# A fused attention-and-MLP kernel: block 1's half of the seven-product groups, one group quarter in SBUF, and a new instruction sequence

## The chip, the cores and the metric

The kernel runs on one core of a Trainium2 chip. TensorE (PE) multiplies into PSUM, which has eight banks of 128 x 512 fp32; VectorE (DVE) and ScalarE (ACT) read and write PSUM and SBUF, GpSimd (POOL) works on SBUF alone; SyncE (SP), ACT and POOL issue DMAs. The metric is the device time in microseconds (us), the median of three executions.

## The reference

Linear attention with random features, then a two-layer MLP with a hard-swish between its layers. With 8 batches, 8 heads, 576 tokens, head size 64, 128 features, hidden size 512 and inner size 2048 it computes, cut to what matters:

```
phi(x) = exp(x' @ omega.T - |x'|^2/2 - max) / sqrt(m)      # x' = x * 64**-0.25
kv, z  = sum over tokens of phi(k) v,  sum of phi(k)
x      = (phi(q) kv) / (phi(q) z + 1e-6)                   # then heads side by side: 4608 x 512
h      = x @ w_in                                          # 4608 x 2048
g      = h * clip(h + 3, 0, 6) / 6
out    = g @ w_out                                         # 4608 x 512
```

## The kernel before

**Tiling.** One batch's first 512 tokens make a block: block b is batch b for b = 0 to 7. The 64 tokens left over of each batch are woven together into block 8. For each block the MLP has a first product, h = x @ w_in, whose activation goes to the tile `gT`, and a second product, g @ w_out. The attention of batch b+1 is interleaved with the MLP of block b, so that PE has work from both.

**Plain first product.** `mm1` (L1083) makes one row of 128 inner units for 512 tokens: four matmuls 128 x 512 into one PSUM bank. ACT then computes relu(h/6 + 0.5) into `tsb` (L1089), and DVE makes min(tsb, 1) * h into `gT` (L1091). Block 0 goes by half blocks (`mm1_half`, L1302).

**First product by seven products.** `mm1_quad` (L1248) makes a group of four such rows, two neighbouring ones in each half of w_in, by seven products of quarter matrices (Strassen's scheme in Winograd's form) in place of eight. A group takes seven times four matmuls 128 x 256, called qa, qw, qb, qy, qz, qc and qd, into four banks X, Y, Z and W. It needs three copies of a bank (q1, q2, q3; ACT or DVE, L543 and L544), two additions on DVE (q4, L1273; q5, L1276), then four times ACT's relu (qr0 to qr3, L1284) and four times DVE's last step (qg0 to qg3, L1286). q3 copies bank W into an SBUF tile `p7`, of which there are two in turn; q5 adds Z and `p7` back into bank W, and qr2 and qg2 read the third quarter there. The scheme also needs sums of w_in, made once per half of the groups (`input_sums`: W3, W2, W4 and W1, the last of which overwrites a quarter of w_in), and four sums of x in each block (`x_sums`: X1 to X4). All such sums are SBUF additions in `combine` (L1343), on DVE or POOL.

`FIRST7 = (7, 2)` and `QUAD = (7, 2)` say from which block on the two halves of the groups (inner units f with f // 4 = 0 and 1) go by seven products: the first half from block 7, the second from block 2. Block 1 is all plain.

**Second product.** From block 1 on it goes by seven products as well (`products`, L1415, 128 x 256), with sums S1 to S4 of `gT` (`token_sums`, `last_sum`; again `combine`, L1343), and with additions on DVE at L1431.

**Attention.** Loads are DMAs: k and q for batches 1 and up are cast on the way by POOL's DMA queue (L643), v comes by SP's. From batch 2 on k and q are transposed by SP's DMA queue (L777), and the attention's output x too (`xT`, L1059, and `xS`). `K`, `Q` and, from batch 3 on, the burst `R` (four row tiles, L796 and L799) project on omega; ACT takes exp (L815, L824; L847, L864 in the early batches), DVE the maxima (L820, L851). `vc` (L970 on POOL, L972 on ACT) scales v, `vcl` (L886 POOL, L889 ACT) v's left over tokens, and `kv` and `num` (L986, L1014) do the sums. DVE divides (L1030).

**What sets the order.** The program builds a list of operations with the data that they read and write. `ORDER` gives, for every engine, the sequence of its operations by their place in that list, so it also says which of several allowed engines does one. `schedule` walks these lists with a table of durations and landing times; what that walk decides is which PSUM bank an operation gets, where idle PE matmuls on the tile `fill` (L597) go in the first microseconds, and in which order waits are recorded. It can't change the sequence of an engine. Each engine then runs its list in order and stands still when the next operation has to wait.

Of the kernel before, what the change touches and what calls it, by code (L numbers as in the profile page):

```python
# [16 lines left out]
EV0 = (("ACT","DVE"), ("ACT","DVE"), ("POOL", "ACT"), {"k": ("POOL", "ACT", "DVE"), "q": ("POOL", "ACT","DVE")})  # L17
# [4 lines left out]
        14, 121, 115, 117, 131, 138, 159, 147, 119, 141, 150, 144, 156, 135, 127, 153, 123, 125, 176, 129, 133, 174,  # L22
        166, 170, 172, 168, 188, 190, 203, 162, 178, 205, 164, 218, 193, 180, 220, 233, 208, 195, 235, 210, 407, 248,
        395, 223, 401, 198, 396, 238, 402, 397, 240, 408, 403, 398, 245, 225, 409, 404, 410, 213, 413, 416, 243, 228,
        271, 419, 291, 251, 422, 425, 428, 431, 275, 281, 434, 277, 437, 279, 318, 440, 443, 273, 309, 446, 315, 306,
        289, 285, 449, 312, 287, 297, 300, 586, 596, 303, 326, 320, 597, 336, 576, 294, 587, 330, 577, 588, 328, 283,
        578, 598, 332, 324, 589, 322, 599, 357, 579, 566, 359, 567, 362, 344, 580, 590, 568, 346, 334, 383, 569, 570,
        571, 349, 370, 385, 591, 365, 572, 581, 375, 372, 388, 600, 601, 592, 582, 583, 352, 391, 593, 573, 378, 602,
        603, 617, 505, 620, 614, 623, 466, 469, 475, 478, 635, 490, 472, 629, 632, 487, 481, 647, 484, 659, 644, 507,
        501, 653, 638, 497, 493, 668, 503, 499, 665, 662, 495, 650, 779, 511, 509, 531, 519, 780, 521, 536, 533, 524,  # L30
        789, 555, 782, 783, 560, 557, 790, 543, 712, 545, 548, 792, 793, 692, 795, 798, 799, 705, 796, 816, 810, 813,
        719, 819, 825, 828, 840, 831, 834, 845, 842, 844, 802, 863, 847, 803, 868, 849, 851, 865, 744, 870, 867, 732,
        987, 874, 737, 997, 734, 988, 872, 768, 756, 746, 1003, 749, 761, 990, 758, 998, 773, 770, 991, 1000, 1001, 900,
        1004, 1006, 1007, 913, 1018, 1024, 1021, 920, 1010, 1027, 1033, 927, 1039, 1050, 1048, 1036, 1011, 1042, 1053,
        1071, 1052, 1073, 1055, 1076, 1057, 1075, 952, 1059, 1078, 1080, 1195, 940, 976, 1082, 942, 957, 1196, 945, 954,
        1205, 964, 1198, 969, 966, 1199, 1206, 978, 981, 1121, 1208, 1209, 1108, 1214, 1215, 1128, 1229, 1232, 1226,
        1241, 1135, 1235, 1244, 1256, 1247, 1250, 1261, 1258, 1260, 1211, 1263, 1279, 1212, 1265, 1284, 1267, 1283,
        1281, 1218, 1286, 1403, 1404, 1290, 1148, 1160, 1219, 1150, 1165, 1288, 1184, 1162, 1153, 1406, 1413, 1414,
        1329, 1189, 1407, 1186, 1172, 1416, 1174, 1177, 1336, 1417, 1419, 1420, 1316, 1422, 1423, 1440, 1437, 1434,
        1452, 1464, 1449, 1443, 1466, 1468, 1469, 1458, 1455, 1471, 1426, 1473, 1427, 1343, 1475, 1487, 1356, 1611,  # L40
        1491, 1492, 1358, 1380, 1489, 1361, 1494, 1382, 1368, 1612, 1370, 1498, 1496, 1373, 1614, 1392, 1621, 1615,
        1622, 1537, 1394, 1397, 1385, 1624, 1625, 1544, 1627, 1628, 1551, 1630, 1634, 1631, 1524, 1635, 1642, 1645,
        1672, 1648, 1651, 1657, 1660, 1677, 1674, 1676, 1663, 1564, 1576, 1679, 1566, 1578, 1569, 1666, 1681, 1695,
        1581, 1683, 1588, 1699, 1600, 1590, 1697, 1593, 1700, 1722, 1702, 1602, 1723, 1605, 1704, 1706, 1753, 1732,
        1725, 1776, 1726, 1733, 1757, 1758, 1755, 1781, 1735, 1760, 1736, 1762, 1764, 1778, 1780, 1783, 1741, 1799,
        1742, 1787, 1785, 1738, 1804, 1801, 1824, 1803, 1806, 1822, 1739, 1808, 1810, 1826, 1827, 1745, 1876, 1829,
        1746, 1831, 1833, 1878, 1845, 1881, 1880, 1901, 1846, 1883, 1899, 1885, 1848, 1904, 1903, 1849, 1887, 1924,
        1906, 1922, 1908, 1855, 1927, 1926, 1856, 1910, 1929, 1945, 1858, 1931, 1949, 1933, 1950, 1859, 1861, 1947,
        1862, 1952, 1864, 1978, 1865, 1956, 1968, 1969, 1868, 1869, 1954, 1979, 1984, 1971, 1981, 1982, 1985, 1972,
        1988, 1989, 1997, 2003, 2000,  # L50
    ],
    "SP": [
        0, 18, 22, 33, 20, 23, 26, 25, 24, 27, 28, 32, 29, 30, 31, 262, 260, 261, 465, 464, 462, 463, 461, 459, 460,
        393, 585, 688, 575, 689, 685, 691, 690, 605, 595, 539, 527, 563, 551, 564, 686, 687, 801, 805, 896, 897, 893,
        898, 899, 740, 752, 764, 776, 894, 895, 1105, 777, 1013, 1106, 1104, 1107, 1009, 948, 960, 972, 984, 1103, 1102,
        1101, 1309, 1312, 1217, 1313, 985, 1314, 1315, 1221, 1311, 1168, 1156, 1192, 1180, 1310, 1520, 1429, 1193, 1523,
        1522, 1521, 1425, 1518, 1364, 1400, 1388, 1376, 1401, 1517, 1519, 1572, 1633, 1584, 1637, 1596, 1608, 1609,
        1744, 1748, 1867, 1871, 1992, 1993, 2005,
    ],
    "ACT": [  # L60
        21, 19, 118, 139, 132, 148, 142, 160, 145, 136, 151, 128, 124, 154, 184, 167, 157, 134, 187, 202, 169, 175, 173,
        171, 163, 179, 232, 219, 177, 165, 234, 181, 209, 411, 405, 399, 417, 244, 420, 292, 426, 414, 429, 423, 276,
        435, 278, 432, 319, 438, 444, 310, 441, 447, 307, 316, 286, 313, 301, 450, 304, 321, 298, 327, 295, 337, 329,
        356, 331, 333, 343, 323, 358, 381, 345, 325, 382, 368, 335, 371, 353, 618, 594, 621, 584, 506, 615, 604, 476,
        470, 624, 473, 479, 636, 467, 633, 488, 648, 630, 491, 485, 645, 530, 508, 660, 502, 482, 654, 639, 504, 669,
        666, 500, 498, 494, 496, 651, 512, 663, 520, 554, 781, 541, 510, 542, 784, 544, 713, 717, 715, 718, 699, 704,
        701, 698, 695, 693, 697, 703, 708, 706, 817, 711, 811, 710, 814, 720, 722, 724, 725, 820, 829, 826, 743, 841,
        832, 835, 843, 852, 727, 864, 728, 869, 854, 856, 866, 745, 858, 875, 767, 733, 755, 754, 881, 879, 989, 769,
        757, 877, 992, 906, 907, 903, 912, 901, 905, 909, 911, 914, 918, 916, 919, 1025, 1019, 1022, 925, 926, 923,
        1028, 921, 1034, 930, 932, 939, 928, 1040, 1051, 933, 1049, 1037, 1043, 1054, 1072, 1060, 1074, 1077, 1062,  # L70
        1064, 1083, 1066, 1085, 941, 977, 1089, 963, 1087, 1197, 965, 1200, 1126, 1124, 1127, 1122, 1120, 1117, 1115,
        1119, 1114, 1111, 1109, 1131, 1113, 1230, 1134, 1233, 1133, 1129, 1227, 1242, 1138, 1141, 1136, 1236, 1245,
        1257, 1248, 1159, 1140, 1251, 1262, 1259, 1280, 1268, 1270, 1272, 1274, 1285, 1291, 1282, 1295, 1297, 1149,
        1161, 1183, 1170, 1293, 986, 1171, 1185, 1334, 1330, 1335, 1332, 1408, 1337, 1339, 1341, 1342, 1325, 1317, 1323,
        1319, 1327, 1441, 1321, 1322, 1328, 778, 1435, 1438, 1465, 1453, 1450, 1444, 1467, 1476, 1470, 1459, 1355, 1456,
        1480, 1478, 1346, 1344, 1482, 1348, 1357, 1349, 1499, 1493, 1381, 1490, 1369, 1503, 1613, 1505, 1501, 1393,
        1616, 1543, 1538, 1542, 1540, 1194, 1545, 1549, 1547, 1550, 1557, 1554, 1556, 1552, 1527, 1525, 1531, 1529,
        1535, 1533, 1643, 1530, 1673, 1646, 1536, 1649, 1652, 1658, 1661, 1678, 1675, 1563, 1684, 1664, 1565, 1577,
        1599, 1686, 1696, 1667, 1589, 1690, 1601, 1707, 1698, 1701, 1688, 1724, 1711, 1713, 1709, 1754, 1727, 1777,
        1765, 1756, 1610, 1782, 1769, 1767, 1771, 1779, 1792, 1788, 1790, 1794, 1805, 1802, 1811, 1823, 1815, 1813,  # L80
        1825, 1828, 1817, 1834, 1840, 1836, 1838, 1879, 1882, 1888, 1847, 1902, 1890, 1892, 1911, 1905, 1894, 1925,
        1850, 1923, 1913, 1915, 1928, 1917, 1934, 1946, 1938, 1940, 1951, 1936, 1957, 1948, 1961, 1963, 1959, 1970,
        1991, 1996, 1995, 1994, 1999, 2002,
    ],
    "DVE": [
# [75 lines left out]
class Prog:  # L161
# [47 lines left out]
    def schedule(self):  # L209
# [83 lines left out]
        while any(lists.values()):  # L293
# [33 lines left out]
            else:  # L327
                free[e] = st + occ
                o.end = free[e]
                if e in o.port:  # L330
                    shared[0] = o.end - (0.07 if e == "POOL" else 0.0)
# [89 lines left out]
def _emit(nc, es, q, k, v, omega, w_in, w_out, out):  # L421
# [112 lines left out]
    def dvet(n):  # L534
        return 0.07 + n / 960.0
# [420 lines left out]
    def pair(b, m, t):  # L956
# [11 lines left out]
        def e_vc(E):  # L968
            if E is not nc.scalar:
                return E.tensor_tensor(vcm[:, :, 0:D], v32[:, m, :, :], cbc, ALU.mult)  # L970
# [641 lines left out]
```

## Time and profile before

| what | value |
|---|---|
| median of 3 runs | 302.28 us (301.57 to 302.39) |
| the profiled execution | 302.46 us, span 300.6 us |
| PE busy | 292.2 us, 97% |
| PE weight loads busy | 222.1 us, 74% |
| DVE busy | 271.4 us, 90% |
| ACT busy | 212.9 us, 71% |
| POOL busy | 206.3 us, 69% |
| granted TensorE clock | 1.000 |

The profile gives the span from the first to the last instruction, each engine's busy time in it, groups of instructions by source line, the waits by who released them, the chain of work that ended last, and a timeline. The span is 1.86 us shorter than the device time of the same execution. Busy times on PE are modelled to the end of each matmul and overlap, so that busy PE isn't PE at its peak; a duration on DVE or ACT overlaps the next instruction's start as well.

### The profile page before, as it was taken

The page shows a single profiled execution, that of the slowest core. Times are in us where ns is not written, and L with a number is a line of the kernel's source. Part 1 is how long each engine was busy: PE and PEld are TensorE (multiplying, and loading weights), DVE is VectorE, ACT ScalarE, POOL GpSimd, SP SyncE. Part 2 cuts the span into 40 slices and gives each one's busy share as a digit, 9 for nine tenths or more (in the row PEclk, how much of TensorE's full clock was granted, in tenths as well). Part 3 has the DMA queues.
Part 4 walks back from the last instruction along what each step waited for, and adds up shares of the span by engine and source line. Part 5 has one row for each costly group of instructions (what it writes and reads, how often), then busy time and mean ns, then how long its engine had stood idle before and what let it go on. Part 6 is the DMA issues. An engine that isn't in the chain of part 4 may idle for free.

```text
span 300.6 us, 7551 instructions
## 1 busy us (share of the span) xinstructions
PE 292.2 (97%) x2899; PEld 222.1 (74%) x2899; DVE 271.4 (90%) x593; ACT 212.9 (71%) x479; POOL 206.3 (69%) x226
## 2 busy tenths in 40 slices
PE   7999999999999999999989999999999999999996
PEld 5688955554884798569736887588757788888885
DVE  4889898889999998999879998999999999997875
ACT  2975899199878992997587776985887576687310
POOL 1664827039898986589939869998279939869711
PEclk9999999999999999999999999999999999999999
DMA  7999999999999997799769898999531600300034
GB/s 234 292 188 168 266 200 127 197 215 155 242 110 234 126 191 138 173 139 196 171 169 172 144 241 129 106 200 220 86 94 57 166 0 3 126 16 0 2 143 140
DMA packets 90100, 44.90 MB, mean 149 GB/s; under 512 B 57936, under 2 KB 87760, under 8 KB 90064
## 3 DMA queue, kind: packets, MB, share of 16 engines
q1 hardware_dynamic: 62064, 30.71, 46.1%
q0 software_dynamic: 26592, 12.46, 33.7%
q10 hardware_dynamic: 1408, 1.25, 1.3%
q8 instruction: 23, 0.38, 0.5%
q14 instruction: 13, 0.11, 0.1%
HBM read 36.73 MB, written 9.44 MB: 154 GB/s over the span
## 4 chain that ended last, share of the span: by engine, by line
PE 81%; DVE 8%; ACT 5%; POOL 5%; issue 1%; POOLq 0%
PE p L1415 29%; PE p L1248 15%; PE p L1083 11%; PE p L1327 5%; PE p L1302 4%; PE p L1014 3%; PE p L986 2%; DVE mx L820 2%; PE p L796 2%; POOL s L1343 2%; PE p L597 2%; ACT kp L847 2%; PE p L860 2%; POOL vc L970 1%; PE p L840 1%; PE p L799 1%
## 5 line engine op out<-in xcount | busy, mean ns | idle before, releaser
L1284 ACT ACTIVATE tsb<-p 128x512 f16<-128x512 f32 x72 | 41.4, 601 | 21.8 <-PE p L1248 12.0
L1083 PE MATMUL p<-xT,wi 128*128 128x512 f16 x224 | 53.1, 379 | 1.8 <-ACT qpT L824 1.4
L1286 DVE SCALAR_TENSOR_TENSOR gT<-tsb,p 128x512 f16<-128x512 f16 x72 | 46.8, 676 | 3.0 <-ACT tsb L1284 2.8
L1415 PE MATMUL p<-wo,gT 128*128 128x256 f16 x368 | 47.0, 273 | 0.0
L1083 PEld LDWEIGHTS p<-xT,wi 128*128 128x128 f16 x224 | 21.3, 98 | 24.9 <-ACT qpT L824 2.1
L1091 DVE SCALAR_TENSOR_TENSOR gT<-tsb,p 128x512 f16<-128x512 f16 x56 | 36.4, 674 | 3.1 <-ACT tsb L1089 2.8
L1415 PEld LDWEIGHTS p<-wo,gT 128*128 128x128 f16 x368 | 34.8, 98 | 4.9 <-issue 0.5
L1089 ACT ACTIVATE tsb<-p 128x512 f16<-128x512 f32 x56 | 33.2, 620 | 7.0 <-PE p L1083 5.3
L543 ACT COPY p<-p 128x512 f32<-128x512 f32 x55 | 32.2, 599 | 4.1 <-PE p L1415 2.0
L970 POOL TENSOR_TENSOR vc<-v,cc 128x512 bf16<-128x512 f32 x27 | 28.7, 1061 | 7.1 <-DVE cc L964 5.2
L824 ACT ACTIVATE qpT<-p 128x512 bf16<-128x512 f32 (+1 forms) x50 | 27.7, 577 | 6.8 <-PE p L799 6.8
L1343 POOL TENSOR_TENSOR gT<-gT,s 128x512 f16<-128x512 f16 x21 | 24.3, 1157 | 12.0 <-PE p L1415 10.6
L1415 PE MATMUL p<-t,gT 128*128 128x256 f16 x256 | 31.8, 273 | 0.4 <-DVE u L1431 0.4
L1343 POOL TENSOR_TENSOR gT<-gT 128x512 f16<-128x512 f16 x24 | 28.2, 1177 | 4.7 <-DVE s L1343 3.2
L815 ACT ACTIVATE kp<-p 128x512 bf16<-128x512 f32 (+1 forms) x50 | 26.8, 571 | 5.9 <-PE p L799 5.6
L820 DVE TENSOR_REDUCE mx<-kp 128x4 f32<-128x512 bf16 (+1 forms) x50 | 29.3, 618 | 0.3 <-ACT kp L815 0.3
L643 POOL DMA_DIRECT2D kb<-in_k_dram x21 | 16.2, 774 | 18.8 <-PE p L1083 18.1
L1030 DVE TENSOR_TENSOR xb<-p,rec 128x384 f16<-128x384 f32 (+1 forms) x64 | 28.2, 467 | 0.3
L1415 PEld LDWEIGHTS p<-t,gT 128*128 128x128 f16 x256 | 24.3, 98 | 5.4 <-issue 1.3
L1343 POOL TENSOR_TENSOR s<-gT,s 128x512 f16<-128x512 f16 x21 | 24.4, 1164 | 3.4 <-DVE s L1343 2.2
L1343 POOL TENSOR_TENSOR s<-gT 128x512 f16<-128x512 f16 x19 | 22.0, 1158 | 4.7 <-DVE gT L1286 3.1
L643 POOL DMA_DIRECT2D qb<-in_q_dram x28 | 19.6, 713 | 7.5 <-PE p L1083 5.0
(139 smaller groups left out, 671.4 us busy)
## 6 DMA issues: line engine op xcount, KB each, us to landing
v<-in_v_dram SPq DMA_DIRECT2D x14, 512.0 KB, 4.8
out_dram<-osb SPq DMA_DIRECT2D x14, 512.0 KB, 3.3
kb<-in_k_dram POOLq DMA_DIRECT2D x14, 256.0 KB, 5.0
qb<-in_q_dram POOLq DMA_DIRECT2D x14, 256.0 KB, 5.6
wo<-in_moe_w_out_dram POOLq DMA_DIRECT2D x8, 256.0 KB, 9.9
wi<-in_moe_w_in_dram POOLq DMA_DIRECT2D x3, 512.0 KB, 7.5
q<-in_q_dram SPq DMA_DIRECT2D x4, 256.0 KB, 4.8
vl<-in_v_dram SPq DMA_DIRECT2D x8, 128.0 KB, 4.2
```

The costliest lines, as they stand in the source:

```text
L543: return E.copy(dst(), src())
L643: lambda E: E.dma_start(dst, src), prio + 0.001 * turn_of[0], reads=gate, writes=keys,
L820: op("DVE", dvet(128 * (d1 - d0)), lambda E, ko=ko, mo=mo: E.reduce_max(mo, ko, axis=AX.X), p0 + 0.01, reads=[("kp", 0, d, lh) for d in ra ...
L970: return E.tensor_tensor(vcm[:, :, 0:D], v32[:, m, :, :], cbc, ALU.mult)
L1083: ins = E.matmul(ring.t[vh.slot], wi[:, c, 128 * f:128 * f + 128], xv[:, c, :], start=(c == 0), stop=(c == NJ - 1))
L1089: op("ACT", actt(512), lambda E: E.activation(tsb[tu][:], ring.t[vh.slot], AF.Relu, bias=0.5, scale=1.0 / 6.0), t - 0.1, reads=[vh], write ...
L1091: op("DVE", dvet(512), lambda E: E.scalar_tensor_tensor(gT[gu][:, f, :], tsb[tu][:], 1.0, ring.t[vh.slot], ALU.min, ALU.mult), t - 0.1, re ...
L1248: ins = E.matmul(bank(v)[:, 256 * g:256 * g + 256], w(c, f + g), x[:, c, :], start=start and g == 0 and c == 0, stop=c == 1, skip_group_ch ...
L1284: op("ACT", actt(512), lambda E, v=v, tu=tu: E.activation(tsb[tu][:], bank(v), AF.Relu, bias=0.5, scale=1.0 / 6.0), t - 0.1, reads=[v], wr ...
L1286: op("DVE", dvet(512), lambda E, v=v, tu=tu, dst=dst: E.scalar_tensor_tensor(dst, pieces(tsb[tu][:]), 1.0, pieces(bank(v)), ALU.min, ALU.m ...
L1343: op(engines, {"POOL": 0.1 + n / 475.0, "DVE": 0.09 + n / 2000.0}, lambda E: E.tensor_tensor(dst, x, y, ALU.subtract if minus else ALU.add ...
L1415: ins = E.matmul(ring.t[v.slot][:, 256 * j:256 * j + 256], a[:, f, 128 * j:128 * j + 128], w[:, f, :], start=(first and f == 0 and j == 0) ...
```

## The change

1. `FIRST7` and `QUAD` become (7, 1): the two groups of the second half in block 1 go by seven products. Block 1 gets `x_sums`. `input_sums` for that half is issued after block 0's first product in place of block 1's.
2. In `mm1_quad`, q5 writes its sum into `p7` in SBUF and not into bank W; qr2 and qg2 read it there. Bank W is free once q3 has copied it.
3. In batch 0, each `vc` is split into two halves, and DVE may do one too.
4. The table of durations is set anew: transposes by DMA land later (`lat` 1.0 to 1.7 for k and q, 1.0 to 2.0 for xT), their issue takes longer, loads from batch 2 on land later, POOL's additions take longer, and qg2 counts as a user of the SBUF port that DVE and POOL share.
5. All five sequences in `ORDER` are new. The number of operations in them, and what changed engine:

| sequence | before | after | of this |
|---|---|---|---|
| PE | 561 | 567 | 14 quad products more, 8 `mm1` fewer |
| SP | 112 | 113 | one output store from ACT |
| ACT | 442 | 464 | q1 +5, q2 +2, `vcc` +7, copies to xS +4, to kT, qT and xT +7, `kvz` -2, stores -1 |
| DVE | 593 | 613 | S1 +7, S3 +5, S4 +2, x sums +7, q4 and q5 +4, q3 +2, q1 -3, `vc` halves +2, `kvz` +2, copies to kT, qT, xT and xS -8 |
| POOL | 222 | 197 | S1 -7, S3 -5, S4 -2, x sums -3, `vcc` -7, copies to xS -3, `vc` +2 (batch 0: six halves for four) |

The `relu` and `g` of block 1's eight plain rows are as many as the qr and qg of its two groups. In block 1 the four x sums are on DVE, all six copies q1 to q3 on ACT, and three of the four S1 too have gone from POOL to DVE. Of block 1's attention, DVE's copies to kT and qT go from seven to four and to xT from three to two; the copy to xS of batch 0 goes from DVE to ACT. In batch 0, `vcl` goes from ACT to POOL and one copy to qT (`Tevq0.1B`) from DVE to ACT.

```diff
-EV0 = (("ACT","DVE"), ("ACT","DVE"), ("POOL", "ACT"), {"k": ("POOL", "ACT", "DVE"), "q": ("POOL", "ACT","DVE")})
+EV0 = (("ACT","DVE"), ("ACT","DVE"), ("POOL", "ACT", "DVE"), {"k": ("POOL", "ACT", "DVE"), "q": ("POOL", "ACT","DVE")})
...
@@ attention: transposes of k and q by DMA
-                       lat=1.0, name="Tdma%s.%d.%d" % (t, b, i), issue=1.42, packet=24.0)
+                       lat=1.7, name="Tdma%s.%d.%d" % (t, b, i), issue=1.5, packet=24.0)
...
@@ pair
-        cbc = bass.AP(cc[pb], c0, [[NCH, 128], [1, 8], [0, D]])
+        def cbc(i0, i1):
+            return bass.AP(cc[pb], c0 + i0, [[NCH, 128], [1, i1 - i0], [0, D]])
+
...
+        for hs in ([0], [1]) if b == 0 else ([0, 1],):
+            i0, i1 = 4 * hs[0], 4 * hs[-1] + 4
+
+            def e_vc(E, i0=i0, i1=i1):
+                if E is not nc.scalar:
+                    return E.tensor_tensor(vcm[:, i0:i1, 0:D], v32[:, m, i0:i1, :], cbc(i0, i1), ALU.mult)
...
-               group="dxT%d_%d" % (pb, m), inc=16, lat=1.0, name="Xdma" + nm, issue=1.27, packet=24.0)
+               group="dxT%d_%d" % (pb, m), inc=16, lat=2.0, name="Xdma" + nm, issue=1.4, packet=24.0)
...
-    FIRST7 = (7, 2)
-    QUAD = (7, 2)
+    FIRST7 = (7, 1)
+    QUAD = (7, 1)
...
@@ mm1_quad
         def bank(v):
-            return v.ring.t[v.slot]
+            return v.ring.t[v.slot] if isinstance(v, Virt) else p7[v[1]][:]
...
-        op("DVE", dvet(512), lambda E: E.tensor_tensor(bank(W), bank(Z), p7[w7][:], ALU.add), t - 0.1, reads=[("p7", w7), Z], writes=[W],
-           name="q5." + nm)
+        op("DVE", dvet(512), lambda E: E.tensor_tensor(p7[w7][:], bank(Z), p7[w7][:], ALU.add), t - 0.1, reads=[Z],
+           writes=[("p7", w7)], name="q5." + nm)
...
-        for n, (v, i, k_) in enumerate(((X, 0, 0), (Y, 1, 0), (W, 1, 1), (Z, 0, 1))):
+        for n, (v, i, k_) in enumerate(((X, 0, 0), (Y, 1, 0), (("p7", w7), 1, 1), (Z, 0, 1))):
...
-               t - 0.1, reads=[v, ("t", tu)], writes=[("gT", gu, 8 * i + f + x, k_) for x in range(2)], name="qg%d.%s" % (n, nm))
+               t - 0.1, reads=[v, ("t", tu)], writes=[("gT", gu, 8 * i + f + x, k_) for x in range(2)], name="qg%d.%s" % (n, nm),
+               port="DVE" if n == 2 else ())
...
@@ combine
-        op(engines, {"POOL": 0.1 + n / 475.0, "DVE": 0.09 + n / 2000.0}, lambda E: E.tensor_tensor(
+        op(engines, {"POOL": 0.157 + n / 475.0, "DVE": 0.08 + n / 2000.0}, lambda E: E.tensor_tensor(
...
@@ the loop over batches, after block 0's mm1_half
+            for h in range(2):
+                if FIRST7[h] == 1:
+                    input_sums(h)
             continue
```

## The prediction

> **What bounds the kernel now.** I read the page first: its first part (busy time per engine) and its fourth (the chain that ended last).
>
> ```profile
> PE 292.2 (97%) x2899; PEld 222.1 (74%) x2899; DVE 271.4 (90%) x593; ACT 212.9 (71%) x479; POOL 206.3 (69%) x226
> ...
> PE 81%; DVE 8%; ACT 5%; POOL 5%; issue 1%; POOLq 0%
> ```
>
> PE carries the time from 1.45 us to the end, with DVE close behind. Then the chain in order of time, for the pace of PE where nothing holds it (start, length, count), and the busy time by stage (stretch, its length, then busy time of PE, PEld, DVE, ACT, POOL):
>
> ```profile
> 104.04 1.75 PE p L1248 x16
> ...
> 186.51 3.45 PE p L1083 x16
> ```
>
> ```profile
> 50.00:60.00 10.00, 10.00 (x98) 5.74 (x94) 9.01 (x25) 2.95 (x11) 1.22 (x2) 1.00 1.36 197
> 60.00:80.00 20.00, 20.00 (x146) 11.60 (x145) 18.36 (x35) 19.34 (x43) 14.02 (x17) 1.00 1.12 194
> 80.00:100.00 20.00, 19.85 (x199) 13.39 (x198) 19.35 (x47) 16.50 (x40) 17.14 (x17) 1.00 1.02 186
> ...
> 150.00:162.00 12.00, 10.21 (x71) 5.06 (x69) 10.22 (x20) 10.04 (x24) 7.21 (x10) 1.00 0.92 162
> ```
>
> A matmul of 256 columns takes 1.75/16 = 0.109 us, one of 512 takes 3.45/16 = 0.216. Block 1's MLP and what surrounds it lie in 50 to 100 us: DVE has 0.99 + 1.64 + 0.65 = 3.3 us idle there. Last I looked at the timeline for the places where PE stood after the start-up; the bracket is the idle time before the instruction and who ended it:
>
> ```profile
> 152.93 3.61 PE L1083 MATMUL p<-xT,wi 128*128 128x512 f16 x16 [1.37 <-ACT qpT L824]
> ...
> 160.65 1.04 PE L1083 MATMUL p<-xT,wi 128*128 128x512 f16 x4 [0.42 <-DVE gT L1091]
> ...
> 238.04 1.03 PE L1415 MATMUL p<-t,s 128*128 128x256 f16 x8 [0.67 <-POOL s L1343]
> ...
> 281.01 1.05 PE L1415 MATMUL p<-t,gT 128*128 128x256 f16 x8 [0.42 <-DVE u L1431]
> ```
>
> These four holes sum to 1.37 + 0.42 + 0.67 + 0.42 = 2.9 us. All else from 25 us on is PE work, so there are only three ways to a shorter time: less PE work, fewer holes, a shorter start.
>
> **What the Trainium skill says.** "TensorE: Matmul & The Clock Gate", Back-to-back issue gap, gives N/2.4 + 2.5 ns for a warm matmul, 109 ns at 256 and 216 at 512 columns; the trace agrees to the nanosecond (above), and not with the same section's 131 ns for sustained 512-column streams. "SBUF — State Buffer", Who interferes with whom: a DVE instruction with two SBUF inputs shuts out a GpSimd instruction that reads SBUF and the other way round, for the whole instruction. The trace agrees: DVE additions in `combine` last 0.41 us alone but 0.49 to 0.64 on the mean, POOL's 1.16. "Perfetto Trace Analysis", Optimizing Scalar/DVE Operations: an access costs DVE about 60 ns on SBUF and 125 on PSUM, ACT 93 and 51. No row of this trace reads fp32 from SBUF in L1284 or L1286, so that stays a price for qg2 and qr2.
>
> **The change, part by part.**
>
> *PE work.* Two groups by seven products add 2 x 7 x 4 = 56 matmuls of 256: 56 x 0.109 = 6.10 us. Eight plain rows go: 8 x 4 = 32 of 512, 32 x 0.216 = 6.91. Net -0.8 us. The code may put a 512-column matmul ahead to clear a bank (two a group, so up to 4 x 0.216 = 0.9 us, which would eat the gain); none of the 18 groups before has one (L597 is the only row on `fill`, all of 256 columns), so I take 0. PE is the bound, so this gain arrives if nothing else gets in the way.
>
> *DVE.* From the rows: S1 +7 at 0.63, S3 +5 at 0.49, S4 +2 at 0.51, x sums +7 at about 0.50 (rows from 0.41 to 0.64), q4 and q5 +4 at 0.69, copies of a bank -1 at 0.69, two `vc` halves (no row; the division of 128x256 takes 0.41), `kvz` +2 at 0.29, and -8 small copies, together -3.3. Sum 4.4 + 2.5 + 1.0 + 3.5 + 2.8 - 0.7 + 0.8 + 0.6 - 3.3 = +11.6 us: 271.4 becomes 283.0, 94% of the span. ACT gets some 12 us (q1 and q2 +7 at 0.60, `vcc` +7 at 0.23, xS +4, small copies +7) and stays at 75%; POOL loses 17 additions at 1.16, 7 `vcc` at 0.26 and 3 copies at 0.79, some 24 us. ACT's and POOL's shares have cover; DVE's hardly has.
>
> *DVE in block 1.* There the two groups and the x sums add 4 x 0.69 + 4 x 0.41 = 4.4 us. The moves in and around it nearly cancel: three S1 come (+1.9) and two x sums of block 2 (+1.0), one S3 goes (-0.5), seven copies to kT and qT become four (-1.0), one to xT and one to xS go (-1.1): +0.3. W1 moves from 88 us to before block 1, inside the stretch. So 4.7 us meet 3.3 us idle: 1.4 us too much. DVE's next work is late by that, behind it the `gT` that block 1's sums and PE's products wait for. Where PE has the slower engine's work in hand nothing is lost (end 0), where it has none, all of 4.7 is (other end); I take 1.0.
>
> *The fourth quarter in SBUF.* Twenty q5, qr2, qg2. By the skill's prices qg2 gets 20 x 0.065 = 1.3 us shorter and qr2 20 x 0.042 = 0.8 longer. qg2 now has two SBUF inputs and can wait for a POOL addition: up to 20 x 1.16 = 23 us on DVE, with POOL busy some 60% and half an instruction left on average 20 x 0.6 x 0.58 = 7, but the other way POOL waits, and the 43 DVE additions of before lost only some 0.15 us each, so I take 20 x 0.15 = 3. That falls on DVE, and of the net 1.7 us hardly anything reaches PE outside blocks 1 and 2. A bank free earlier is worth something only where PE waits for a bank. I take 0 for the two together, between -0.5 and +1.5.
>
> *Start-up.* `vcl` leaves ACT, where the chain had it ("12.91 1.05 ACT vcl L889 x4"), one copy to qT comes (0.59): -0.4 us, since ACT is full from 10 to 20 us. It can be 0 if the loads end that stretch. POOL takes `vcl` (2 x 0.62), with six `vc` halves for four whole ones behind it.
>
> *The sequence.* Landings to xT took 2.4 to 6.1 us, median 3.1; POOL lost 8.7 us in two waits for them (the row "POOL x L1343 <- DMA xT<-xb"), and the hole at 238 is POOL's row of back-to-back work from 222 on. The new lists read landed tiles later, and 17 additions of 1.16 us have left POOL: the hole at 238 (0.67) should go. The one at 153 hangs on ACT emptying the banks of three R bursts; the new list has two R in a row there, so I give it no more than half. No DMA is added; one store changes queue, off the path. Of 2.9 us I take half, -1.5; the ends are -2.9 and, with new holes, +2.
>
> Sum: -0.8 + 1.0 + 0 - 0.4 - 1.5 = -1.7 us. The profiled execution took 302.46 us (span 300.6, 1.86 around it): 300.8. It lay 0.2 above the median of 302.28; from the median it is 300.6, which I predict.
>
> **Rivals.**
>
> *All holes close.* With -2.9 for the holes, DVE's surplus covered and the 0.8 and 0.4: -4.1, so 298.2. For it: POOL is relieved and PE is never held for long before. Against it: a new sequence has its own holes, and DVE is fuller.
>
> *Nothing gained.* The landing times only change a plan; holes come back elsewhere, and PE's 0.8 pays for DVE's delays. About 302.2. For it: before's holes are 1% of the span, as any sequence may have.
>
> *DVE becomes the bound between 60 and 120 us (slower).* PE waits in its order behind q4, q5 and the qg of blocks 1 and 2, and what it loses isn't made up. Price: all 4.7 us of block 1's surplus, qg2's 3 us of port waits with a fifth of them in these blocks (0.6), against -0.8, -0.4 and -1.5: +2.6, so 304.9; with a hole or two fewer 304. It decides once PE's waits for DVE there exceed 2.7 us, the sum of the three gains. For it: DVE is at 18.4 and 19.4 of 20 us. Against it: half of block 1's plain work is replaced one for one.
>
> **How the numbers follow.** The forecast 0.45, with a range of its own from 299.4 to 301.4; all holes close 0.15; nothing gained 0.15; DVE the bound 0.25. Within 0.3% (301.4 to 303.2), about what a measurement can't tell from no change, lies the third case: faster 0.60, same 0.15, slower 0.25. From 298.0 to 304.3 there is all of the first three but a tail, and half of the fourth.
>
> **What would show it.** PE matmuls 2899 + 24 but for the idle ones on `fill`; L1248 with 560 of them, L1083 with 192. DVE at 281 to 286 us, POOL near 182. PE's first matmul of L1302 some 0.4 us earlier than 20.1 us. No hole of over 0.3 us at the start of block 7's seven products; half of the others gone. Wrong if PE shows waits for DVE of over 2 us in 60 to 120 us, if L1286's mean rises over 0.75 us (port), or if `fill` appears under L1248's helper.

## The result and the profile after

The change makes the kernel slower: 303.41 us median of 6 runs (303.27 to 304.27) against 301.62 for the kernel before (301.20 to 302.39) on the same chip, ratio 1.0056, 95% interval 1.0037 to 1.0076. The prediction was 300.6. The profiled execution of the kernel after took 304.27 us (span 302.5), the slowest of its six, and that of before 302.46 (span 300.6). Below, lines of `kernel.py` are those of the kernel after: what was L1083, L1091, L1248, L1273, L1276, L1286, L1343, L1415 and L1431 is now L1090, L1098, L1255, L1280, L1283, L1293, L1351, L1423 and L1439.

The page of the kernel after, busy time by engine:

```profile
PE 292.9 (97%) x2927; PEld 225.8 (75%) x2927; DVE 278.6 (92%) x613; ACT 220.6 (73%) x502; POOL 185.4 (61%) x201
```

2927 matmuls are 2899 + 24, as worked out, and four more of the idle ones at the start. The chain that ended last covers only 28% of this span on its page, so it serves here for PE's pace alone (start, length, count):

```profile
221.96 4.32 PE p L1090 x20
...
237.05 1.75 PE p L1255 x16
```

4.32/20 = 0.216 and 1.75/16 = 0.109 us, as before: PE's work did fall by 0.8 us. The busy times by stage (columns as in the prediction):

```profile
50.00:60.00 10.00, 10.00 (x100) 5.87 (x99) 8.32 (x23) 4.79 (x12) 1.03 (x2) 1.00 1.28 174
60.00:80.00 20.00, 20.00 (x172) 14.07 (x171) 19.88 (x43) 19.73 (x48) 13.63 (x16) 1.00 1.09 205
80.00:100.00 20.00, 20.00 (x212) 14.29 (x209) 19.73 (x49) 17.14 (x42) 11.41 (x12) 1.00 0.79 164
150.00:162.00 12.00, 11.20 (x89) 6.84 (x86) 11.13 (x26) 11.27 (x25) 6.39 (x8) 1.00 0.50 86
```

From 50 to 100 us, where the change adds its seven products, PE has no idle time at all, though DVE is at 19.9 and 19.7 of 20 us. The places where PE stands lie elsewhere. From the timeline of PE (in the bracket the idle time before the instruction and who ended it):

```profile
104.68 1.05 PE L1255 MATMUL p<-q,wi 128*128 128x256 f16 x8 [0.70 <-DVE p L1280]
...
153.53 0.40 PE L796 MATMUL p<-om,kT 64*128 64x128 bf16 x8 [0.78 <-ACT kp L815]
...
164.82 0.61 PE L1255 MATMUL p<-xT,wi 128*128 128x256 f16 x4 [1.05 <-DVE gT L1098]
...
183.56 1.92 PE L1423 MATMUL p<-t,gT 128*128 128x256 f16 x16 [0.47 <-DVE gT L1351]
...
219.17 1.05 PE L1423 MATMUL p<-wo,gT 128*128 128x256 f16 x8 [0.54 <-DVE gT L1351]
...
257.06 0.61 PE L1255 MATMUL p<-x,k 128*128 128x256 f16 x4 [0.37 <-DVE gT L1293]
```

Three of before's four holes are gone (160, 238 and 281 us) and the one at 153 fell from 1.37 to 0.78: 2.1 us won. But five new ones, of 3.1 us together, all end on DVE. What DVE did ahead of two of them, with POOL beside it:

```profile
102.72 1.28 DVE L1351 TENSOR_TENSOR gT<-gT 128x512 f16<-128x512 f16 x1
103.93 0.69 DVE L1280 TENSOR_TENSOR p<-p,p 128x512 f32<-128x512 f32 x1
...
102.69 2.23 POOL L975 TENSOR_TENSOR vc<-v,cc 128x512 bf16<-128x512 f32 x2
...
162.25 1.91 DVE L1351 TENSOR_TENSOR q<-xT,q 128x512 f16<-128x512 f16 x1
164.09 0.68 DVE L1098 SCALAR_TENSOR_TENSOR gT<-tsb,p 128x512 f16<-128x512 f16 x1
...
162.67 1.20 POOL L1351 TENSOR_TENSOR s<-gT 128x512 f16<-128x512 f16 x1
```

The row sum S12.0 takes 1.28 us, not 0.41, and behind it stands q4.2.4 (L1280), for which PE waits. The x sum X4.4 takes 1.91, and behind it stands the `g` (L1098) that empties PE's next bank. It is likewise at the other three (P4.4 and P5.6 belong to the second products of blocks 4 and 5, qw.8.2 to the first of block 8): S14.2 and S14.0 take 0.75 and 1.37 ahead of P4.4 (S44.0 behind them takes 1.37 too, but P4.4 doesn't wait for it), S45.3 takes 1.35 in the queue ahead of P5.6, and qg2.7.2 takes 1.67 ahead of the bank that qw.8.2 needs.

By the distance of PE's matmuls from one another, less the pace of their row, the holes cost 3.7 us before and 5.1 after, of which the five new ones 3.9 (a bracket shows 0.15 to 0.4 less than the hole costs). With -0.8 of work, +0.5 at 20 us, +0.7 at a load of k that came late at 30.4 us (a_mend, below, has the same order there and no such wait) and +0.35 behind PE's last product this gives +2.1; the span grew by 1.9.

### The profile page after: what moved, and what is told of

The parts are those of the page before. It is cut to its first block, busy times and chain, and to the rows that moved or that the text cites. A ratio compares the mean times of both kernels' runs of the same rounds, so it can differ in the third digit from the quotient of the medians.

```text
span 302.5 us, 7643 instructions
## 1 busy us (share of the span) xinstructions
PE 292.9 (97%) x2927; PEld 225.8 (75%) x2927; DVE 278.6 (92%) x613; ACT 220.6 (73%) x502; POOL 185.4 (61%) x201
## 5 line engine op out<-in xcount | busy, mean ns | idle before, releaser
L1293 DVE SCALAR_TENSOR_TENSOR gT<-tsb,p 128x512 f16<-128x512 f16 x80 | 53.8, 696 | 1.4 <-ACT tsb L1291 1.1
L1291 ACT ACTIVATE tsb<-p 128x512 f16<-128x512 f32 x80 | 46.3, 613 | 11.8 <-DVE gT L1293 5.6
L1423 PE MATMUL p<-wo,gT 128*128 128x256 f16 x368 | 47.1, 273 | 0.5 <-DVE gT L1351 0.5
L1090 PE MATMUL p<-xT,wi 128*128 128x512 f16 x192 | 46.5, 379 | 0.0
L543 ACT COPY p<-p 128x512 f32<-128x512 f32 x63 | 36.9, 607 | 11.3 <-PE p L1423 5.4
L1423 PEld LDWEIGHTS p<-wo,gT 128*128 128x128 f16 x368 | 34.6, 98 | 5.7 <-DVE gT L1351 0.8
L975 POOL TENSOR_TENSOR vc<-v,cc 128x512 bf16<-128x512 f32 (+1 forms) x29 | 28.1, 968 | 9.5 <-DVE cc L964 6.0
L1096 ACT ACTIVATE tsb<-p 128x512 f16<-128x512 f32 x48 | 29.6, 640 | 5.2 <-PE p L1090 3.0
L1351 POOL TENSOR_TENSOR gT<-gT,s 128x512 f16<-128x512 f16 x19 | 22.8, 1203 | 16.3 <-PE p L1423 10.5
L1351 POOL TENSOR_TENSOR s<-gT,s 128x512 f16<-128x512 f16 x21 | 25.7, 1225 | 10.7 <-DVE s L1351 8.2
L1098 DVE SCALAR_TENSOR_TENSOR gT<-tsb,p 128x512 f16<-128x512 f16 x48 | 31.5, 674 | 0.5 <-ACT tsb L1096 0.4
L1090 PEld LDWEIGHTS p<-xT,wi 128*128 128x128 f16 x192 | 18.4, 98 | 17.8 <-ACT qpT L824 0.7
L1423 PE MATMUL p<-t,gT 128*128 128x256 f16 x256 | 31.0, 273 | 0.6 <-DVE gT L1351 0.5
L1037 DVE TENSOR_TENSOR xb<-p,rec 128x256 f16<-128x256 f32 (+1 forms) x64 | 28.4, 469 | 0.2
L1423 PEld LDWEIGHTS p<-t,gT 128*128 128x128 f16 x256 | 24.3, 98 | 5.5 <-issue 1.1
L1351 POOL TENSOR_TENSOR gT<-gT 128x512 f16<-128x512 f16 x17 | 20.4, 1201 | 4.8 <-DVE s L1351 2.0
L1351 POOL TENSOR_TENSOR s<-gT 128x512 f16<-128x512 f16 x14 | 17.5, 1248 | 5.4 <-DVE gT L1293 2.9
```

The costliest lines, as they stand in the source:

```text
L543: return E.copy(dst(), src())
L1037: op("DVE", dvet(128 * n), lambda E: E.tensor_tensor(xv(i0, i1), psum()[:, :, :, 0:64], rbc, ALU.mult), t + 0.01, reads=[vn, ("rec", ru)], ...
L1090: ins = E.matmul(ring.t[vh.slot], wi[:, c, 128 * f:128 * f + 128], xv[:, c, :], start=(c == 0), stop=(c == NJ - 1))
L1096: op("ACT", actt(512), lambda E: E.activation(tsb[tu][:], ring.t[vh.slot], AF.Relu, bias=0.5, scale=1.0 / 6.0), t - 0.1, reads=[vh], write ...
L1098: op("DVE", dvet(512), lambda E: E.scalar_tensor_tensor(gT[gu][:, f, :], tsb[tu][:], 1.0, ring.t[vh.slot], ALU.min, ALU.mult), t - 0.1, re ...
L1291: op("ACT", actt(512), lambda E, v=v, tu=tu: E.activation(tsb[tu][:], bank(v), AF.Relu, bias=0.5, scale=1.0 / 6.0), t - 0.1, reads=[v], wr ...
```

## The experiments

All are compared with runs of the kernel before on the same chip; the kernel after stands at 1.0056 on this scale. The experiments ran on three chips, where before's median was 301.91, 302.07 and 302.29, so rows are best compared by their ratios. Spans are of the profiled executions.

| kernel | median us | ratio to before, 95% | span us |
|---|---|---|---|
| after | 303.41 | 1.0056 (1.0037 to 1.0076) | 302.5 |
| a_mend | 300.70 | 0.9966 (0.9951 to 0.9980) | 298.7 |
| a_start | 302.54 | 1.0015 (1.0003 to 1.0027) | 300.7 |
| a_block0 | 303.90 | 1.0063 (1.0040 to 1.0085) | 302.6 |
| a_block0_mend | 301.43 | 0.9989 (0.9977 to 1.0001) | 299.1 |
| a_start_mend | 300.57 | 0.9951 (0.9936 to 0.9966) | 299.0 |
| b_mend | 301.36 | 0.9977 (0.9960 to 0.9994) | 299.9 |
| b_seven | 303.52 | 1.0057 (1.0035 to 1.0080) | 301.8 |
| a_mend_bank | 313.72 | 1.0394 (1.0370 to 1.0417) | 312.2 |
| a_port | 300.08 | 0.9916 (0.9897 to 0.9935) | 298.7 |
| a_best | 300.02 | 0.9924 (0.9900 to 0.9947) | 298.1 |
| b_seven_late | 303.17 | 1.0029 (1.0018 to 1.0039) | 301.2 |

**a_mend: eight DVE instructions in other places.** DVE's list of the kernel after, in names for its numbers:

```diff
-g.2.3 S12.0 q4.2.4 g.2.11 g.2.10 q5.2.4 kvz.3.1
+g.2.3 q4.2.4 g.2.11 g.2.10 q5.2.4 S12.0 kvz.3.1
...
-q4.4.4 ccl.5 g.4.1 g.4.2 X4.4 g.4.9
+X4.4 q4.4.4 ccl.5 g.4.1 g.4.2 g.4.9
...
-mx6.6.0 S14.2 S14.0 S44.0 u3.4
+S14.0 S14.2 mx6.6.0 u3.4 S44.0
...
-u3.5 mx7.6.0 mx7.6.1 mx7.10.1 C22.5 S45.0
+u3.5 S45.0 mx7.6.0 mx7.6.1 mx7.10.1 C22.5
...
-q4.7.4 qg2.7.2 qg3.7.2
+q4.7.4 qg3.7.2 qg2.7.2
```

In these names `g.` is the last step of a plain row, `mx` a maximum, `u` and `C` additions of the second product, `ccl` a reciprocal.

> The kernel after, with eight instructions of VectorE moved to other places in its own list, and nothing else: S12.0 (a row sum of block 2) behind q5.2.4 instead of ahead of q4.2.4; X4.4 ahead of q4.4.4; S14.0 first, then S14.2, and mx6.6.0 and S44.0 behind them; S45.0 ahead of the two mx7.6; qg3.7.2 ahead of qg2.7.2. They stood ahead of the instruction that TensorE waited for in the five holes of the kernel after at 104.7 us (0.7), 164.8 (1.05), 183.6 (0.47), 219.2 (0.54) and 257.1 (0.37), together 3.1 us. Theory 1, the loss is a queue of VectorE instructions that happen to stand in the wrong place: most of the 3.1 comes back, 2.0 to 3.0 us, so 300.4 to 301.4. Rival, VectorE's 278.6 us of work are the bound and a hole that is closed opens again elsewhere: at most 0.8 us comes back, so 302.6 or more.

Measured: 300.70 us, ratio 0.9966, so 0.9% or 2.7 us less than the kernel after, and faster than before. Theory 1 holds. PE's holes in the timeline of a_mend from 100 us on:

```profile
109.18 0.61 PE L1256 MATMUL p<-xT,q 128*128 128x256 f16 x4 [0.21 <-DVE p L1284]
...
152.57 0.40 PE L797 MATMUL p<-om,kT 64*128 64x128 bf16 x8 [0.79 <-ACT kp L816]
...
216.04 1.05 PE L1424 MATMUL p<-wo,gT 128*128 128x256 f16 x8 [0.54 <-DVE osb L1440]
```

(Lines are one higher in this kernel.) Four of the five are closed; at 216 us PE now waits for another instruction, C22.5. The excess of DVE's row and x sums and of qg2 over their undisturbed time fell from 9.6 to 6.3 us, so this run changes both things at once, the place and the meeting with POOL. a_port separates them.

**a_port: POOL's instructions beside those sums cut short, all lists as they are.**

```diff
     def combine(name, dst, x, y, minus, n, prio, reads, writes, engines=ADD):
+        if name in ("S34.0", "S44.2", "X1.5", "S44.3", "S45.1", "S37.0"): dst, x, y = dst[:, :, 0:8], x[:, :, 0:8], y[:, :, 0:8]
...
+                    if nm in (".3.0", ".3.1"): i1 = i0 + 1
                     return E.tensor_tensor(vcm[:, i0:i1, 0:D], v32[:, m, i0:i1, :], cbc(i0, i1), ALU.mult)
```

The kernel leaves out most of the columns of eight instructions, so it doesn't compute the reference; it is there for its time alone. (Its lines are up to two higher.)

> The kernel after with every list as it is, but eight of GpSimd's instructions cut to a fraction of their columns: S34.0, S44.2, X1.5, S44.3, S45.1 and S37.0 add 16 columns, not 512, and vc.3.0 and vc.3.1 multiply one group of 64 columns, not eight. They leave the rest of their sums out. Each is the instruction of GpSimd beside which a sum of VectorE, the one just ahead of a hole, took 1.28 (S12.0), 1.91 (X4.4), 0.75, 1.37 and 1.37 (S14.2, S14.0, S44.0), 1.35 (S45.3) and 1.67 us (qg2.7.2), where a sum of VectorE alone takes 0.416 (41 of them, none over 0.425) and qg2 0.68. Theory 1, what makes the holes is the wait of VectorE for GpSimd's instruction to end: those sums fall to 0.42 to 0.45, the holes at 104.7, 164.8, 183.6 and 257.1 close or nearly so, 2.0 to 3.0 us faster than the kernel after: 300.4 to 301.4, with VectorE's list untouched. Rival, the place in the list alone is enough, 0.4 us of a sum where TensorE waits: less than 1.0 us comes back, 302.4 or more.

Measured: 300.08 us, ratio 0.9916, 1.4% or 4.2 us less than the kernel after. DVE in its timeline at the two places shown above:

```profile
102.45 0.54 DVE L1353 TENSOR_TENSOR gT<-gT 128x512 f16<-128x512 f16 x1
102.91 0.69 DVE L1281 TENSOR_TENSOR p<-p,p 128x512 f32<-128x512 f32 x1
...
161.24 0.42 DVE L1353 TENSOR_TENSOR q<-xT,q 128x512 f16<-128x512 f16 x1
161.57 0.68 DVE L1099 SCALAR_TENSOR_TENSOR gT<-tsb,p 128x512 f16<-128x512 f16 x1
```

And all holes of PE from 100 us on:

```profile
152.51 0.40 PE L796 MATMUL p<-om,kT 64*128 64x128 bf16 x8 [0.78 <-ACT kp L815]
...
267.68 0.61 PE L1256 MATMUL p<-q,wi 128*128 128x256 f16 x4 [0.31 <-DVE p L1281]
```

With DVE's list untouched the sums are back at 0.54 and 0.42 us and the five holes are gone. So it is DVE's wait for POOL's instruction, and not the 0.41 us of a sum in the wrong place, that makes them; the rival falls. The 4.2 us are near the 3.9 that the five holes cost by the distance of PE's matmuls; POOL itself is busy for 178.2 instead of 185.4 us here, and what that adds isn't separated. One wait is not POOL's sum alone: X4.4 of the kernel after begins at 162.25 us, while POOL issues a transfer (161.92 to 162.69), and 0.42 us before POOL's sum S34.0 begins.

**a_start and a_block0: the order of before at the start.**

```diff
-        for hs in ([0], [1]) if b == 0 else ([0, 1],):
+        for hs in ([0, 1],):
```

and in `ORDER` all that the plan of before begins in its first 22 (a_start) or 50 us (a_block0), then the rest as after.

> The kernel after, with the order of before for all that begins in the first 22 us of the plan, and vc of batch 0 whole again (four multiplications of 512 columns, not eight halves); the rest stands in the order of after. Theory 1, part of the loss is the start-up: TensorE's lateness was 0.5 us greater at 20 us and 0.9 at 35 us, so 0.5 to 0.9 us comes back: 302.5 to 302.9. Rival, the start-up has slack behind it (loads land when they land): 303.3 to 303.5, and TensorE is as late at 50 us as in the kernel after.

> As a_start, but with the order of before up to 50 us of the plan, that is for the whole of block 0 and the start of block 1's attention. Theory 1: the 1.15 us that TensorE was later at 50 us come back, 302.1 to 302.5, of which a_start gives the first 0.5 to 0.9. Rival: all of that is made good again by waits that grow later, 303.0 or more.

a_start: ratio 1.0015, 0.4% less than after, 0.9 us by the medians and 1.2 by the ratios, at the upper end of theory 1 or above it. But not all of that need be the start-up. In the profile of a_start the hole at 104.7 us (0.70) is gone too, though no list changed there and S12.0 still stands ahead of q4.2.4 (DVE, then POOL; lines one higher):

```profile
101.76 0.42 DVE L1352 TENSOR_TENSOR gT<-gT 128x512 f16<-128x512 f16 x1
102.10 0.69 DVE L1281 TENSOR_TENSOR p<-p,p 128x512 f32<-128x512 f32 x1
...
101.84 2.36 POOL L976 TENSOR_TENSOR vc<-v,cc 128x512 bf16<-128x512 f32 x2
```

In the kernel after S12.0 began 0.04 us after POOL's `vc` and waited for all of it; here it began 0.08 us before it and took 0.42, and POOL's first `vc` took 1.24 us in place of 1.04. That is a third witness for the port, and it makes a_start a weak measure of the start-up. a_block0 gains nothing (1.0063), against its theory 1: between 50 and 60 us of its profile PE lost another 1.2 us at the seam of the two orders, and the hole at 104.9 us (0.71) is there, so it says nothing of block 0. In the profile of the kernel after, the last half of `vc` stands on POOL behind the issue of a load (18.35 us, 0.80 long), its product begins at 20.21 us, and the first MLP product at 20.5 us, where before it was 20.1. That this half is what a_start wins back was not tried by itself.

**a_block0_mend and a_start_mend: both sorts together.**

> a_block0 and a_mend together. Theory 1, the losses are places in the order that do not depend on one another: their sum comes back, 3.1 to 4.1 us, so 299.3 to 300.3, which is faster than the kernel before. Rival, VectorE's work is the bound: the gains don't add, and the time stays above that of the kernel before, 301.6.

> a_start and a_mend together: the order of before for the first 22 us with vc of batch 0 whole, and the eight VectorE instructions of a_mend moved. Theory 1, places that do not depend on one another: the 0.9 to 1.2 us of a_start and the 2.7 us of a_mend add up, 299.5 to 299.9, faster than before by 2 us. Rival, they share a slack, as a_block0 and a_mend seem to do: no better than a_mend, 300.5 or more.

a_block0_mend: 0.9989, between its two theories, with the seam's loss on top of a_mend. a_start_mend: 0.9951 against a_mend's 0.9966, with intervals that overlap; the two gains add by 0.15%, not by 0.4%, and its 300.57 us lie with the rival. In its profile PE was 0.7 us later at 25 us than in a_start, with the same order up to there, so the start-up varies from execution to execution by as much as the gain in question. Where the holes are mended in both kernels, then, the start-up is worth 0.15%, some 0.5 us, which isn't clear of noise; what a_start shows beyond that can be the hole at 104.7 us.

**b_mend: the same remedy for the kernel before.**

```diff
 DVE
-X3.4 g.4.0 mx5.10.0 X4.4 mx5.0.0 g.4.2
+X3.4 g.4.0 mx5.10.0 g.4.2 X4.4 mx5.0.0
...
-S28.1 u3.7
+u3.7 S28.1
 POOL
-S36.1 S36.2 S26.1
+S36.1 S26.1 S36.2
```

> The kernel before, with three instructions moved in the same way and nothing of the change: g.4.2 ahead of X4.4 on VectorE (the hole at 160.7 us, 0.42), S26.1 ahead of S36.2 on GpSimd (238.0, 0.67), u3.7 ahead of S28.1 on VectorE (281.0, 0.42), together 1.5 us. Theory 1, holes are places in the lists, in either kernel: 1.0 to 1.6 us faster than before, 300.0 to 300.6, and then the change itself, mended in both kernels, is worth no more than PE's 0.8 less the start-up. Rival, before's holes are the limits of its engines and move elsewhere: 301.2 or more.

Measured: 0.9977, 0.7 us, between the two. Its two largest holes:

```profile
152.99 3.61 PE L1083 MATMUL p<-xT,wi 128*128 128x512 f16 x16 [1.03 <-ACT kp L815]
...
239.91 1.05 PE L1415 MATMUL p<-wo,gT 128*128 128x256 f16 x8 [0.50 <-DVE gT L1286]
```

Two of the three are closed; the one at 238 us has only passed from POOL to DVE. In the trace of before the two closed ones stood behind long sums as well: X4.4, beside POOL's issues of transfers, ahead of g.4.2, and S28.1, beside a POOL addition, ahead of u3.7:

```profile
158.33 1.33 DVE L1343 TENSOR_TENSOR q<-xT,q 128x512 f16<-128x512 f16 x1
...
278.94 1.41 DVE L1343 TENSOR_TENSOR s<-gT,s 128x512 f16<-128x512 f16 x1
```

So DVE's wait for POOL, which makes the new holes, could be read from before's own trace, at two of the four holes that the prediction lists. Against b_mend, a_start_mend is at 0.9951/0.9977 = 0.9974, that is 0.8 us less, as much as the saved PE work. The two intervals (0.9936 to 0.9966 and 0.9960 to 0.9994) touch, so the agreement may be chance; and it is a comparison of one mending of each, not a proof that nothing else is left.

**b_seven and b_seven_late: part one alone, on the kernel before.**

```diff
-    FIRST7 = (7, 2)
-    QUAD = (7, 2)
+    FIRST7 = (7, 1)
+    QUAD = (7, 1)
```

with `input_sums` placed as in the change, the order of block 1 taken over and then rearranged between 36 and 115 us (b_seven) or 36 and 150 us (b_seven_late) of the plan. The rest is before's, the fourth quarter in its bank too.

> The kernel before with part one of the change alone: the first half of block 1's MLP by seven products, with the order between 36 and 115 us of the plan arranged for it, and the order of before everywhere else; the fourth quarter stays in its bank, vc of batch 0 whole. TensorE has 0.8 us less work. Theory 1, the products come free of waits as they did in the kernel after: 0.5 to 1.0 us faster than before, 300.6 to 301.1. Rival of the prediction, VectorE's 4.7 us more in a stretch where it had 3.3 us idle hold TensorE: 301.8 to 304.

> b_seven with the order of its stretch (36 to 150 us of the plan) arranged against the later landings of the kernel after (2.0 us for a transposing transfer to xT and 1.7 to kT and qT, both 1.0 before), and nothing else changed: in the plan block 3's first product stood 0.01 us behind the landing of its xT in b_seven, and stands 1.6 us behind it here. Theory 1, b_seven lost its 0.8 us and more because its order counted on landings that the chip doesn't keep (TensorE waited 1.03 us for xT at 124.5 and 0.38 for qT at 119.4): 1.0 to 1.8 us faster than b_seven, 301.7 to 302.5. Rival, part one itself costs time in a sequence made for plain products: 303.0 to 304.

b_seven: 1.0057, 1.7 us slower than before, in the range of the rival. b_seven_late: 1.0029. The two differ by 0.28%, 0.8 us, less than theory 1 said, and its 303.17 us lie in the rival's range. In the timeline of b_seven PE waits for ACT's copy of a bank in block 1, with ACT and DVE both busy for all of 60 to 80 us, and later for a landing:

```profile
76.14 0.61 PE L1248 MATMUL p<-q,wi 128*128 128x256 f16 x4 [0.27 <-ACT p L543]
...
124.52 1.67 PE L1083 MATMUL p<-xT,wi 128*128 128x512 f16 x7 [1.03 <-DMA xT<-xb]
```

None of b_seven's holes between 50 and 130 us ends on DVE, so the rival has the time, but PE's waits are not for DVE itself. In b_seven_late the wait for the landing is gone, the one for ACT is 0.46 us, and another hole has come:

```profile
96.12 0.40 PE L796 MATMUL p<-om,kT 64*128 64x128 bf16 x8 [0.55 <-DVE gT L1091]
```

So planning with later landings does take the waits for landings away here; but an order rearranged for one part brings holes of its own. The brackets don't add up to what the two kernels lose (the hole at 153 us, 1.37 before, is gone in both). Whether part one alone could give its 0.8 us in an order without such holes, or needs the bank that part two frees, stays open.

**a_mend_bank: part two undone in five blocks of a_mend.**

```diff
+        V4 = W if blk in (1, 2, 3, 5, 6) else ("p7", w7)
-        op("DVE", dvet(512), lambda E: E.tensor_tensor(p7[w7][:], bank(Z), p7[w7][:], ALU.add), t - 0.1, reads=[Z],
-           writes=[("p7", w7)], name="q5." + nm)
+        op("DVE", dvet(512), lambda E: E.tensor_tensor(bank(V4), bank(Z), p7[w7][:], ALU.add), t - 0.1, reads=[Z] + ([("p7", w7)] if V4 is W else []),
+           writes=[V4], name="q5." + nm)
...
-        for n, (v, i, k_) in enumerate(((X, 0, 0), (Y, 1, 0), (("p7", w7), 1, 1), (Z, 0, 1))):
+        for n, (v, i, k_) in enumerate(((X, 0, 0), (Y, 1, 0), (V4, 1, 1), (Z, 0, 1))):
...
```

> a_mend with part two of the change undone in blocks 1, 2, 3, 5 and 6: there q5 writes its sum into the bank that held q3's product, and qr2 and qg2 read it there, as in the kernel before; the lists stay those of a_mend. (In blocks 4, 7 and 8 these lists can't run without the freed bank.) Theory A, the freed bank is worth nothing to TensorE, as the prediction had it: within 0.5 us of a_mend, 300.2 to 301.2, or up to 1 us faster where the port waits of 12 of the 20 qg2 go. Theory B, the new lists lean on the freed bank: 2 us slower than a_mend or more, with the waits at first products (qw, qa) whose bank isn't free.

Measured: 313.72 us, 13 us slower than a_mend. Two of its holes, of which the timeline shows sixteen:

```profile
109.69 0.60 PE L1255 MATMUL p<-q,k 128*128 128x256 f16 x4 [1.26 <-DVE kvz L544]
...
204.14 0.40 PE L796 MATMUL p<-om,kT 64*128 64x128 bf16 x8 [1.85 <-DVE gT L1098]
```

Theory B by its size, though the waits are not only at qw and qa: the first line is a qy, which needs a fourth bank for its group, the second a burst R, and five of the sixteen end on ACT. The new lists lean on the freed bank. That is not yet a gain over an order made for a bank that isn't freed: the kernel before ran without it at 301.6.

**a_best: one more DVE instruction.** a_start_mend and

```diff
-S45.0 mx7.6.0 mx7.6.1 mx7.10.1 C22.5
+S45.0 mx7.6.0 C22.5 mx7.6.1 mx7.10.1
```

> a_start_mend with one more VectorE instruction moved: C22.5 (it empties a bank) ahead of mx7.6.1 and mx7.10.1. In a_mend and a_start_mend TensorE still waits 0.54 us at 216 us, now for C22.5, which starts 0.7 us after its own product has ended, behind two maxima. Theory 1: the 0.54 us come back, 299.6 to 300.1 where a_start_mend had 300.4. Rival, the next wait takes its place: 300.3 to 300.7.

Measured: 300.02 us, ratio 0.9924; against a_start_mend 0.27%, 0.8 us, with intervals that overlap. Faster than both kernels, by 0.8% and 1.3%. DVE and then PE at that place:

```profile
210.43 1.35 DVE L1351 TENSOR_TENSOR gT<-gT,s 128x512 f16<-128x512 f16 x1
...
213.70 0.67 DVE L1439 TENSOR_TENSOR osb<-p,u 128x512 f32<-128x512 f32 x1
...
214.92 1.04 PE L1423 MATMUL p<-wo,gT 128*128 128x256 f16 x8
```

PE no longer waits there, as theory 1 said. The sum at 210.43 (S45.3) is held by POOL for 0.9 us just as in the kernel after, and costs nothing, since nothing that PE needs soon stands behind it.

## Why the prediction was wrong

*PE work, -0.8: right.* The counts and paces are as predicted, no matmul on `fill` went to a product's bank, and block 1 took the gain without a hole.

*DVE, +11.6 to 283.0: too much.* It is 278.6. I priced the 21 additional row and x sums by means of rows that contain waits for POOL (0.49 to 0.63 us); alone they take 0.416. At 0.416 the 21 cost 8.7 us, not 11.4, which is 2.7 of the 4.4 us; the rest wasn't traced.

*DVE in block 1, +1.0: did not occur.* DVE did 47.9 us of work from 50 to 100 us where it did 46.7, and PE stood for none of it. Of the 4.7 us that I counted into the stretch 1.2 show there. In before's order (b_seven) it was ACT, whose share I thought covered, that PE waited for in this stretch.

*The fourth quarter in SBUF, 0: within its range as far as it shows, most terms not.* qg2 is not shorter with fp32 from SBUF: 17 of the 20 took 0.65 to 0.69 us, and before the rows with a PSUM input had a mean of 0.676; the 0.065 us that I took from the Trainium skill ("Perfetto Trace Analysis", Optimizing Scalar/DVE Operations) don't show. The price for ACT does: qr2 took 0.641 us on the mean where it took 0.600 before, 0.8 us over the twenty as predicted. The waits for POOL came to 1.6 us, not 3, in three of 20 instructions, and only one of them, qg2.7.2, lay in front of a hole (0.37). The freed bank I put at nothing; the new lists can't do without it (a_mend_bank).

*Start-up, -0.4: wrong sign.* PE's first MLP product came 0.4 us later, not earlier. The step counted ACT's relief and not that POOL's halves of `vc` get a load's issue between them; that this is the reason is read from one trace and wasn't tried. With the holes mended the start-up costs some 0.5 us, not clear of noise.

*The sequence, -1.5: the step that failed.* It had two terms. Old holes: I expected half of 2.9 us back and got 2.1, the one at 238 among them. New holes: I put them at nothing in the sum, and only the outer end of +2 allowed for them. They came to 3.1 us in brackets, and closing them is worth 2.7 us (a_mend) to 4.2 (a_port). Without them the terms roughly add up: -0.8 of work, -2.1 of old holes and some +0.5 at the start make -2.4, and a_port stands at 0.9916, -2.5 us. That a_mend's 300.70 is next to the 300.6 that I predicted is luck: against the kernel before it gains 1.0 us, not 1.7. Why they came is in a sentence of the fourth-quarter step: DVE's additions "lost only some 0.15 us each" to POOL. That is a mean over two kinds. In the trace of before 24 sums that met a computation of POOL took 0.75 us on the mean and up to 1.41, the other 31 took 0.411 and never over 0.425; after, 22 took 0.76 and up to 1.91. The number of meetings and their excess over the undisturbed time changed little (8.2 us before, 9.6 after with qg2). What changed is where they fall: ahead of instructions for which PE waits at five places, where it was two before (160 and 281 us, b_mend). The Trainium skill says in "SBUF — State Buffer", Who interferes with whom, that the one that comes second is blocked for the whole instruction; I quoted it and then priced it as an average.

*The rivals of the prediction.* "Nothing gained" had holes come back elsewhere and PE's 0.8 us pay for DVE's delays, and is nearest: it gave 302.2 where before stood at 302.28, no change, and the kernel is 0.56% slower. "DVE becomes the bound between 60 and 120 us" had the right engine and the wrong place and mechanism: PE's waits for DVE there were 0.70 us, against the 2.7 that it needed. DVE is not short of time in the kernel after: a_mend leaves it the same instructions and is 2.7 us faster.

## What to carry to other kernels

A wait for a port shared by two engines is to be priced at the place where it falls, by its longest and not by its mean: list the SBUF-only DVE instructions that stand just ahead of what the bounding engine waits for, see what POOL does beside each, and count a whole POOL instruction where they meet. Such a hole can come or go with 0.1 us of timing, so its absence from one trace (a_start) is no proof that a kernel is free of it. A new order of a kernel is a change by itself, worth more here than the work that was saved, so ask of each new hole whether one instruction moved closes it before blaming the engine's load. And an order made for a buffer can't be read without it: taking one away from a finished order tells of that order, not of the buffer.

## What was not expected of the hardware

- When a DVE sum began 0.04 to 0.13 us after a POOL computation, it ended 0.27 to 0.28 us after POOL's end: S12.0, S14.0, S44.0, S35.1 and S45.3, which took 1.25 to 1.37 us in place of 0.416. When it began up to 0.05 us before, it took 0.41 to 0.43, and POOL's addition 1.39 to 1.42 in place of 1.15: S21.3, S25.3, S16.1 and S17.1. A head start of some hundredths of a microsecond decides on 0.9 us. At 0.03 us it went either way for qg2.7.2: 1.67 us in the kernel after, 0.68 in a_start and a_block0.
- POOL's issues of transfers mostly did not do this, but they can: 13 sums of the kernel after that met only such issues took 0.434 us on the mean, one of them 0.74. X4.4 of before took 1.33 us from 158.33 on, while POOL issued transfers until 159.53 and began a computation only at 159.50; in b_mend it took 0.74 beside such issues.
- A POOL addition of 16 columns took 0.22 to 0.26 us in a_port (the one that qg2.7.2 held, 0.78), one of 512 that nothing held 1.15 to 1.2.
- `qg` took the same 0.68 us with its fp32 input from SBUF as from PSUM; ACT's `qr` took 0.64 from SBUF and 0.60 from PSUM.
